# First heads loaded one at a time over two queues, products on zeros before them, last sums finished one after the other

## The chip, the cores and the metric

The kernel runs on one core of a Trainium2 chip. The metric is device time in microseconds (us) for one launch; less is better. A core has five engines that run side by side, each with its own queue of instructions in a fixed order: TensorE (PE, matrix products), VectorE (DVE), ScalarE (ACT), GpSimd (POOL), and SyncE (SP), which here issues DMAs. 16 DMA engines move the data.

## The reference

Attention with capped scores, then two feed-forward stages on its output:

```python
scores = cap * tanh(scale * (q @ k.T) / cap)          # 4 batches, 12 heads, 448 positions, 64 wide
attn = softmax(scores)
x = (attn @ v)                                        # 1792 tokens, 768 wide
h = x @ w_in;  g = h * cos(h);  x = g @ w_out          # 768 -> 2048 -> 768
out = ((x @ w1) * (x @ w2)) @ w3 @ w_out2              # 768 -> 1024 -> 1024 -> 768
```

All inputs are float32. For a `cap` above 40 the softmax needs its maximum taken off; a general form of the program does that.

## The kernel before

The kernel splits float32 operands into two parts, high and low (`qh`, `ql`, `xh`, `xl` and so on), in a type that TensorE multiplies at one column per cycle, and sums two or three products of the parts. Four pieces of work follow one another and overlap:

- *Attention.* 48 heads, each in two steps, 96 steps in all. A step is four products of q and k (`c_S`, lines 574 and 575) into one of two double banks, a tanh and an exp on ACT (`c_exp`, line 584, tiles `double` and `p`), and two float32 products with v (`c_PV`, line 595), which the trace shows as four records. Heads come in pairs: q and k of a pair are loaded into `qr` and `kr`, each by two DMAs of 64 partitions (the same rows once to each half), and split into `qh`, `ql` and `ks`.
- *Weights w3 by w_out2.* `make_w34` multiplies them on TensorE (lines 357 to 359, 384 columns, tiles `w3h`, `w2h`), between attention steps. Raw weights arrive as 64-bit numbers (`raw`), and ACT, POOL and DVE turn them into parts.
- *The first feed-forward stage*, `moe1`, begins beside the second half of attention.
- *The second*, `moe2`: for each batch and each of eight columns `fc`, `ab_unit` makes the two factors and `o_unit` adds their product with the joint weights (`w34`) into six sums. The factor's two parts, `abh` and `abl`, are made by DVE while `o_unit` of the column before runs. At the last column each sum is copied by ACT or DVE to `ob` (a ring of three buffers) and written to `outT` by a DMA.

The order of work on each engine is set ahead of time by a planner (`Plan.schedule`): every operation has a due time and a set of engines that can do it, the planner walks through time with its own costs and picks the most urgent operation that is ready, and what comes out is the order of each engine's queue. The engines then run in that order, each waiting where an operand isn't there. `PAR` holds the numbers that set the due times: attention step `g` is due at `t0 + g * p1` (10.0 and 3.4), and from step 48 on at a slower pace. The weights w3 by w_out2 are due from 20.0 on (`wb`).

All DMAs are issued by SP. The first is `capt`, the cap, then q of the first pair, k of the first pair, three raw weights and v. The first pair is due before everything else, and the buffers `qr` and `kr` are single (`nq=1`). After the program, `tile_kernel` loads the cap once more, compares it with 40 and reads the result into a register of each engine (lines 299 to 303); a branch on it ends the stream of each engine, jumping over the general form. The scheduler of the framework put the DMA and the comparison in the midst of the run, and the register loads wherever each engine's stream ended, but for SP, which reads it in the midst.

Of the kernel before, what the change touches and what calls it, by code (L numbers as in the profile page):

```python
# [10 lines left out]
F32 = mybir.dt.float32  # L11
# [3 lines left out]
ALU = mybir.AluOpType  # L15
# [97 lines left out]
class Plan:  # L113
# [157 lines left out]
    p1=3.4, p2=6.2, gsw=48, t0=10.0,  # L271
# [8 lines left out]
    nq=1, nqh=2, nph=2, npl=2,  # L280
# [3 lines left out]
    p1=1.98, p2=2.86, gsw=90, t0=14.13, ql=10, qs=4, hsw=26, wb=(30.36, 107.61), we=(108.65, 207.54),  # L284
    m0=222.0, ua=13, pa=19.15, pu=14.2, nt=9, nph=3,
# [4 lines left out]
def tile_kernel(tc, *args):  # L290


    nc = tc.nc
    cap = args[3]
    program(tc, *args)
    with tc.tile_pool(name="large", bufs=1) as p:
        c = p.tile([1, 2], F32, name="cap2")
        large = p.tile([1, 1], mybir.dt.int32, name="large")
        nc.sync.dma_start(c[:, 0:1], cap.rearrange("(o n) -> o n", o=1))
        nc.vector.tensor_scalar(c[:, 1:2], c[:, 0:1], -1.0, None, op0=ALU.mult)  # L300
        nc.vector.tensor_tensor(c[:, 0:1], c[:, 0:1], c[:, 1:2], op=ALU.max)
        nc.vector.tensor_scalar(large, c[:, 0:1], CAP_MAX, None, op0=ALU.is_gt)
        with tc.If(nc.values_load(large[0:1, 0:1], min_val=0, max_val=1) > 0):
            program(tc, *args, general=True)
# [3 lines left out]
def program(  # L308
# [43 lines left out]
    def dma(due, dst, src, r=(), w=(), kb=115, write=False):  # L352
        plan.op(due, [("SP", 0.66, lambda: SP.dma_start(dst(), src()))], r=r, w=w,  # L353
                kb=kb)
# [88 lines left out]
    SP.dma_start(capt, cap.rearrange("(o n) -> o n", o=1).to_broadcast([P, 1]))  # L443
    pac = const([P, 1], "pac")
    DVE.tensor_scalar(nac, capt, -1.0, None, op0=ALU.mult)
    DVE.tensor_tensor(pac, nac, capt, op=ALU.max)
    DVE.tensor_tensor(nac, nac, capt, op=ALU.min)
    DVE.reciprocal(ts, nac)
    DVE.tensor_scalar(ts, ts, -1.0 / math.sqrt(D), None, op0=ALU.mult)
    warm = const([P, 1], "warm")  # L450
    DVE.memset(warm, 0.0)
    ACT.activation(warm, warm, AF.Tanh)
# [23 lines left out]
    def at(g):  # L476

        return G["t0"] + min(g, G["gsw"]) * G["p1"] + max(g - G["gsw"], 0) * G["p2"]
# [9 lines left out]
    def a_load(i, g):  # L488
        b, h = divmod(i, H)
        qk[i] = A["qr"].new(), A["kr"].new()  # L490
        for it, src in zip(qk[i], (q2, k2)):
            for j in range(2):
                r = it.at(j, rows(j))
                dma(at(g) if i else -99.0, r, lambda src=src: src[b, h // 2].rearrange("(i d) s -> d i s", i=2),
                    w=[r], kb=230)

# [63 lines left out]

    def cv_load(i, g):
# [3 lines left out]
        dma(at(g), vt[i][:, :, j, :], lambda: v[b, h], w=[vt[i]])  # L565
# [61 lines left out]

    def columns():
        c_consts()
        a_load(0, -2)  # L630
        a_split(0, -1)
# [130 lines left out]
    def queries():  # L762
        a_load(0, -2)
# [268 lines left out]
    def moe2():  # L1032
        raw_r, x_r = ring("lp", "rawl", [P, 2 * DM], U32, 2), ring("lp", "xl_", [P, DM], F32, 2)
        a_r, ob_r = ring("qp", "a32", [P, S], F32, 2), ring("qp", "ob", [P, S], F32, 3)
# [34 lines left out]
        def o_unit(n, b, fc, due):  # L1069
            abh, abl = ab.pop((b, fc))  # L1070
            wh, wl = w34t[fc]
            for m in range(KD):
                if fc == 0:
                    acc[m] = hy_r.ref()
                o = acc[m]

                def f(o=o, m=m):
                    mm3(o()[:, :S], wh()[:, m * P:(m + 1) * P], wl()[:, m * P:(m + 1) * P], abh(), abl(),
                        fc == 0, fc == NF2 - 1)

                plan.op(due + m * 0.55, [("PE", 3 * MM, f)], r=[wh, wl, abh, abl], w=[o])
                if fc == NF2 - 1:
                    ob = ob_r.ref()
# [79 lines left out]
```

## Time and profile before

| What | us |
|---|---|
| Median of three runs (lowest, highest) | 1142.9 (1142.64, 1143.47) |
| The profiled execution | 1141.23 |
| Its span, first to last instruction | 1139.2 |
| TensorE busy | 1112.9, 98% of the span |
| VectorE, ScalarE, GpSimd busy | 740.5, 454.2, 133.3 |
| First product of the run starts | 10.29 |

The profile shows one execution. Its own time is 2.0 us more than its span, and 1.7 us less than the median of the runs. A busy share is an average over the whole run; what bounds a stretch is read from the waits and the timeline of that stretch. TensorE has two clock levels, 1.2 and 2.4 GHz; the profile has a column for the clock that was granted. It reads 1.00 (the upper level) for the first 28 us of this run, where the spacing of the products says otherwise in part; the prediction goes by the spacing there.

### The profile page before, as it was taken

The numbers are of one execution on the slowest core, as the hardware profiler recorded it, in microseconds if no ns is written. First come the engines' busy times: TensorE is split into PE (matmuls) and PEld (weight loads), VectorE is DVE, ScalarE is ACT, GpSimd is POOL, SyncE is SP. The second block draws the span as 40 slices with busy tenths as digits, with TensorE's granted clock in tenths as the row PEclk, the third lists the DMA queues.
The fourth block names the chain that finished last, engine by engine and source line by source line (L and its number), as shares of the span: only waits on it lengthen the run. The fifth ranks groups of instructions, "written<-read, shape, count | busy, mean of one in ns | idle before, by whom it ended". The sixth has DMA issues, their size and how long they took to land.

```text
span 1139.2 us, 13718 instructions
## 1 busy us (share of the span) xinstructions
PE 1112.9 (98%) x5184; PEld 966.5 (85%) x5184; DVE 740.5 (65%) x1111; ACT 454.2 (40%) x581; POOL 133.3 (12%) x130
## 2 busy tenths in 40 slices
PE   5999999999999999999999999999999999999997
PEld 3777777778888888889999999998999999999996
DVE  5888777899998897787899877768831311311111
ACT  4887767877566655722454211113211101101001
POOL 2312111123231110110121000001200000000000
PEclk9999999999999999999999999999999999999999
DMA  8885765878756554337745211101401101101001
GB/s 231 229 224 149 212 185 171 231 210 252 209 154 188 190 148 158 130 100 235 272 127 180 70 56 56 29 1 69 140 15 41 57 1 41 57 1 40 10 1 51
DMA packets 83165, 140.10 MB, mean 123 GB/s; under 512 B 35986, under 2 KB 63634, under 8 KB 83090
## 3 DMA queue, kind: packets, MB, share of 16 engines
q1 hardware_dynamic: 83090, 139.14, 40.7%
q8 instruction: 42, 0.69, 0.2%
q14 instruction: 33, 0.27, 0.1%
HBM read 109.45 MB, written 29.58 MB: 122 GB/s over the span
## 4 chain that ended last, share of the span: by engine, by line
PE 93%; DVE 2%; DMA 1%; ACT 1%; SPq 1%; issue 0%; POOL 0%; ACTq 0%; DVEq 0%
PE bank L357 13%; PE bank L358 13%; PE bank L359 13%; PE double L358 12%; PE double L359 12%; PE double L357 12%; PE bank L595 12%; PE double L574 3%; PE double L575 3%; DMA rawc<-in_w_out 1%; SPq L353 1%; DMA kr<-in_k 0%; DVE w L343 0%; ACT double L584 0%; ACT p L584 0%
## 5 line engine op out<-in xcount | busy, mean ns | idle before, releaser
L343 DVE TENSOR_TENSOR a<-double,a 128x448 f32<-128x448 f32 x32 | 20.0, 625 | 240.1 <-PE double L359 237.7
L595 PE MATMUL bank<-p,v 112*128 112x448 f32 x384 | 161.3, 543 | 0.5 <-issue 0.5
L359 PE MATMUL double<-xh,w12l 128*128 128x448 f32 x378 | 137.8, 365 | 0.0
L358 PE MATMUL double<-xl,w12h 128*128 128x448 f32 x378 | 137.8, 365 | 0.0
L357 PE MATMUL double<-xh,w12h 128*128 128x448 f32 x378 | 137.4, 363 | 0.0
L584 ACT ACTIVATE double<-double,ts 112x896 f32<-112x896 f32 x96 | 94.1, 981 | 79.1 <-PE double L575 78.9
L333 ACT COPY a<-double 128x448 f32<-128x448 f32 x31 | 16.5, 533 | 254.1 <-PE double L359 254.1
L357 PE MATMUL bank<-xh,wih 128*128 128x448 f32 x270 | 107.9, 399 | 0.0
L595 PEld LDWEIGHTS bank<-p,v 112*128 112x128 f32 x384 | 72.6, 190 | 41.2 <-issue 38.3
L357 PE MATMUL bank<-gh,woh 128*128 128x448 f32 x260 | 102.1, 393 | 0.3 <-ACT hs L333 0.3
L358 PE MATMUL bank<-xl,wih 128*128 128x448 f32 x270 | 98.3, 364 | 0.0
L359 PE MATMUL bank<-xh,wil 128*128 128x448 f32 x270 | 98.0, 363 | 0.0
L584 ACT ACTIVATE p<-double,pac 112x896 f32<-112x896 f32 x96 | 96.7, 1010 | 2.0
L358 PE MATMUL bank<-gl,woh 128*128 128x448 f32 x260 | 95.2, 366 | 0.0
L359 PE MATMUL bank<-gh,wol 128*128 128x448 f32 x260 | 94.8, 365 | 0.0
L574 PE MATMUL double<-qh,ks 128*112 128x448 f32 x192 | 73.7, 384 | 14.4 <-DVE ks L343 10.3
L343 DVE TENSOR_TENSOR y<-bank,y 128x448 f32<-128x448 f32 x111 | 68.6, 619 | 23.0 <-PE bank L359 22.2
L358 PEld LDWEIGHTS double<-xl,w12h 128*128 128x128 f32 x378 | 71.0, 188 | 5.8
L357 PEld LDWEIGHTS double<-xh,w12h 128*128 128x128 f32 x378 | 70.8, 187 | 5.6
L359 PEld LDWEIGHTS double<-xh,w12l 128*128 128x128 f32 x378 | 71.0, 188 | 5.0
L575 PE MATMUL double<-ql,ks 128*112 128x448 f32 x192 | 72.1, 375 | 0.0
L357 PEld LDWEIGHTS bank<-xh,wih 128*128 128x128 f32 x270 | 50.8, 188 | 9.0 <-issue 5.0
(153 smaller groups left out, 2359.2 us busy)
## 6 DMA issues: line engine op xcount, KB each, us to landing
rawc<-in_w_out SPq DMA_DIRECT2D x16, 768.0 KB, 5.6
rawl<-in_w SPq DMA_DIRECT2D x16, 768.0 KB, 4.4
qr<-in_q SPq DMA_DIRECT2D x48, 224.0 KB, 4.6
kr<-in_k SPq DMA_DIRECT2D x48, 224.0 KB, 4.9
rawc<-in_w_in SPq DMA_DIRECT2D x13, 768.0 KB, 5.0
raw<-in_w3T SPq DMA_DIRECT2D x16, 512.0 KB, 5.8
raw<-in_w_out SPq DMA_DIRECT2D x8, 768.0 KB, 7.2
wo_d<-wx SPq DMA_DIRECT2D x16, 384.0 KB, 4.4
```

The lines of the kernel that those rows point to most:

```text
L333: "A": ("ACT", (0.051 if psum else 0.094) + n / 1200, lambda: ACT.copy(dst(), src())),
L343: "D": ("DVE", 0.068 + n / 960, lambda: DVE.tensor_tensor(dst(), a(), b(), op=op))
L353: plan.op(due, [("SP", 0.66, lambda: SP.dma_start(dst(), src()))], r=r, w=w, kb=kb)
L357: PE.matmul(out, wh, xh, start=first, stop=False)
L358: PE.matmul(out, wh, xl, start=False, stop=False)
L359: PE.matmul(out, wl, xh, start=False, stop=last)
L574: PE.matmul(o, w, qh(), start=True, stop=False)
L575: PE.matmul(o, w, ql(), start=False, stop=True)
L584: lambda f=f, x=x, o=o: ACT.activation(o(), s(), f, scale=x[:CP]))],
L595: PE.matmul(pv()[:, :S], w()[:, 2 * c + n].rearrange("p a d -> p (a d)"), p()[:, n, :], start=c == 0 and n == 0, stop=c == NT - 1 and n == 1)
```

## The change

- *Loads of the first pair.* `a_first` takes the place of `a_load(0)` and `a_split(0)`: head 0 and head 1 get DMAs of their own (64 partitions by 448, half the bytes each), k over SP and q over ACT. ACT also issues the cap and v of head 0. ACT copies k's high part, DVE makes the other three parts, head by head. `qr` and `kr` become double (`nq=2`), and the second pair (heads 2 and 3) is loaded right behind the first instead of behind raw weights.
- *Products on zeros.* `c_warm` clears part of the tile `rb` and multiplies it five times (float32, 224 columns) into a bank that nothing reads, ahead of the first real product.
- *Pace.* The first ten attention steps are due every 2.4 (`p0`) instead of 3.4, from 6.5 instead of 10.0.
- *Last sums.* The last two calls of `o_unit` are one: sum by sum, column 6 and then column 7 of a sum, as far as the planner finds the factor of column 7 made. `ob` has four buffers. Writes to `outT` may be issued by SP or ACT.
- *The flag.* The second load of the cap and its three operations are gone; the flag is made from `pac` inside the program, and every engine reads it into its register where the plan's time passes 600.

```diff
-    p1=3.4, p2=6.2, gsw=48, t0=10.0,
+    p0=2.4, p1=3.4, p2=6.2, g0=10, gsw=48, t0=6.5,
...
-    nq=1, nqh=2, nph=2, npl=2,
+    nq=2, nqh=2, nph=2, npl=2,
...
-    program(tc, *args)
-    with tc.tile_pool(name="large", bufs=1) as p:
-        c = p.tile([1, 2], F32, name="cap2")
-        large = p.tile([1, 1], mybir.dt.int32, name="large")
-        nc.sync.dma_start(c[:, 0:1], cap.rearrange("(o n) -> o n", o=1))
...
-        with tc.If(nc.values_load(large[0:1, 0:1], min_val=0, max_val=1) > 0):
-            program(tc, *args, general=True)
+    with tc.If(program(tc, *args) > 0):
+        program(tc, *args, general=True)
...
+            "S": ("SP", 0.66, lambda: SP.dma_start(dst(), src())),
+            "A": ("ACT", 0.66, lambda: ACT.dma_start(dst(), src())),
...
+            DVE.tensor_scalar(large, pac[0:1], CAP_MAX, None, op0=ALU.is_gt)
...
+        g0, g1 = G["g0"], G["gsw"]
+        return G["t0"] + min(g, g0) * G["p0"] + min(max(g - g0, 0), g1 - g0) * G["p1"] + max(g - g1, 0) * G["p2"]
...
-                dma(at(g) if i else -99.0, r, lambda src=src: src[b, h // 2].rearrange("(i d) s -> d i s", i=2),
+                dma(at(g) if i > 2 or general else -97.0, r, lambda src=src: src[b, h // 2].rearrange("(i d) s -> d i s", i=2),
...
+    def a_first():
...
+        for n in range(2):
+            for it, src, e in ((k, k2, "S"), (q, q2, "A")):
+                for j in range(2):
+                    r = it.at((n, j), lambda t, n=n, j=j: t[j * D:(j + 1) * D, n])
+                    dma(-99.0 + n, r, lambda src=src, n=n: src[0, 0, n * D:(n + 1) * D], w=[r], on=e)
...
+            plan.op(due, [("ACT", 0.47, lambda n=n, o=ks_: ACT.copy(o(), k.tile()[:, n]))], r=kj, w=[ks_])
...
+    def c_warm():
+
+        z = A["rb"].tile(0)
+        DVE.memset(z[:, :S // 2], 0.0)
+        for _ in range(5):
+            PE.matmul(banks[7][:, :S // 2], z[:, :P], z[:, :S // 2], start=True, stop=True)
...
-        dma(at(g), vt[i][:, :, j, :], lambda: v[b, h], w=[vt[i]])
+        dma(at(g) if i > 1 else -60.0, vt[i][:, :, j, :], lambda: v[b, h], w=[vt[i]], on="S" if i else "A")
...
-        a_r, ob_r = ring("qp", "a32", [P, S], F32, 2), ring("qp", "ob", [P, S], F32, 3)
+        a_r, ob_r = ring("qp", "a32", [P, S], F32, 2), ring("qp", "ob", [P, S], F32, 4)
...
+            for m in range(KD):
+                for fc, abh, abl, wh, wl in fcs:
...
+                    plan.op(due, [("PE", 3 * MM, f)], r=[wh, wl, abh, abl], w=[o])
+                    due += 0.55
...
-                if prev is not None:
-                    o_unit(*prev, due)
...
+                if prev and (n, fc) != (B - 1, NF2 - 1):
+                    o_unit(prev[0], prev[1], prev[2:], due)
...
+    for t, f in plan.schedule():
+        if over is None and not general and t > 600:
+            over = nc.values_load(large[0:1, 0:1], min_val=0, max_val=1)
```

The change alters due times, so the planner writes another order. Three places follow; the numbers behind names are buffers.

SP at the start, before: the cap, the first pair, weights, then v.

```order
L443 DMA capt<-in_cap 128x1
L353 DMA qr_111<-in_q 64x2x448 x2
L353 DMA kr_114<-in_k 64x2x448 x2
L353 DMA raw_117<-in_w3T 128x1024
L353 DMA raw_119<-in_w_out 128x1536
L353 DMA raw_121<-in_w_out 128x1536
L353 DMA v_103<-in_v 112x4x64
L353 DMA v_107<-in_v 112x4x64
L353 DMA v_105<-in_v 112x4x64
```

All of these stood on one queue. The same, after.

```order
L344 DMA kr_118<-in_k 64x448 x4
L344 DMA qr_128<-in_q 64x2x448 x2
L344 DMA kr_133<-in_k 64x2x448 x2
L344 DMA v_114<-in_v 112x4x64
L344 DMA raw_142<-in_w3T 128x1024
L344 DMA raw_147<-in_w_out 128x1536
L344 DMA raw_151<-in_w_out 128x1536
L344 DMA v_112<-in_v 112x4x64
L344 DMA kr_118<-in_k 64x2x448 x2
L344 DMA qr_121<-in_q 64x2x448 x2
```

The cap, q of the first pair and v of head 0 left SP; the second pair (`qr_128`, `kr_133`) and one v came ahead of the three raw weights.

ACT at the start, before.

```order
L452 ACT_TABLE_LOAD
L452 ACTIVATE warm<-warm 128x1
L804 ACTIVATE raw_117<-raw_117 128x512
L584 ACTIVATE double_75<-double_75,ts 112x2x448
L584 ACTIVATE double_76<-double_76,ts 112x2x448
L584 ACTIVATE p_153<-double_75,pac 112x896
L584 ACTIVATE p_157<-double_76,pac 112x896
L584 ACTIVATE double_75<-double_75,ts 112x2x448
```

No DMA stood on ACT, and a raw weight came ahead of the first tanh of a score. The same, after.

```order
L436 DMA capt<-in_cap 128x1
L345 DMA qr_121<-in_q 64x448 x4
L442 ACT_TABLE_LOAD
L442 ACTIVATE warm<-warm 128x1
L345 DMA v_110<-in_v 112x4x64
L511 CAST ks_138<-kr_118 128x448 x2
L614 ACTIVATE double_75<-double_75,ts 112x2x448
L614 ACTIVATE double_76<-double_76,ts 112x2x448
L614 ACTIVATE p_173<-double_75,pac 112x896
L614 ACTIVATE p_179<-double_76,pac 112x896
L614 ACTIVATE double_75<-double_75,ts 112x2x448
L843 ACTIVATE raw_142<-raw_142 128x512
```

ACT now issues six DMAs before its first tanh, the last of them v of head 0 (`v_110`), which stands between the warming tanh and the two casts of k.

PE at the end, last column 7 (`w34h7`) of the last batch, before: six products on columns 6 and 7 out of the last 36.

```order
L357 MATMUL bank4_77<-abh0_5578,w34h60_5813 128x448
L358 MATMUL bank4_77<-abl0_5590,w34h60_5813 128x448
L359 MATMUL bank4_77<-abh0_5578,w34l60_5822 128x448
L357 MATMUL double1_76<-abh0_5578,w34h60_5813 128x448
L358 MATMUL double1_76<-abl0_5590,w34h60_5813 128x448
L359 MATMUL double1_76<-abh0_5578,w34l60_5822 128x448
L357 MATMUL bank5_78<-abh1_5627,w34h70_5890 128x448
L358 MATMUL bank5_78<-abl1_5633,w34h70_5890 128x448
L359 MATMUL bank5_78<-abh1_5627,w34l70_5892 128x448
L357 MATMUL bank7_80<-abh1_5627,w34h70_5890 128x448
L358 MATMUL bank7_80<-abl1_5633,w34h70_5890 128x448
L359 MATMUL bank7_80<-abh1_5627,w34l70_5892 128x448
```

The last two sums get column 6 and the first two column 7. The same place, after.

```order
L350 MATMUL double1_76<-abh1_5659,w34h70_5922 128x448
L351 MATMUL double1_76<-abl1_5665,w34h70_5922 128x448
L352 MATMUL double1_76<-abh1_5659,w34l70_5924 128x448
L350 MATMUL bank6_79<-abh0_5610,w34h60_5845 128x448
L351 MATMUL bank6_79<-abl0_5622,w34h60_5845 128x448
L352 MATMUL bank6_79<-abh0_5610,w34l60_5854 128x448
L350 MATMUL double0_75<-abh0_5610,w34h60_5845 128x448
L351 MATMUL double0_75<-abl0_5622,w34h60_5845 128x448
L352 MATMUL double0_75<-abh0_5610,w34l60_5854 128x448
L350 MATMUL bank6_79<-abh1_5659,w34h70_5922 128x448
L351 MATMUL bank6_79<-abl1_5665,w34h70_5922 128x448
L352 MATMUL bank6_79<-abh1_5659,w34l70_5924 128x448
```

Before, all six sums get column 6 and then all six get column 7. Now four sums are finished with column 7 before the last two begin with column 6.

## Rows read from the trace of the kernel before

**Rows 1.** Waits of TensorE, whole run: engine, line, releaser; total us, times, longest.
```profile
PE double L574 <- DVE ks L343: 10.3, 1, 10.3
PE double L574 <- ACT p L584: 4.1, 2, 2.1
PE double L358 <- DVE gl L343: 2.6, 1, 2.6
```

**Rows 2.** Timeline of SyncE's queue, first 12 us: start, us, engine, line, operation.
```profile
0.74 0.40 SPq L443 DMA_DIRECT2D capt<-in_cap  x1
1.19 1.39 SPq L353 DMA_DIRECT2D qr<-in_q  x2
...
5.52 5.84 SPq L353 DMA_DIRECT2D v<-in_v  x4
```

**Rows 3.** Timeline of VectorE, first 12 us; in brackets idle before and its releaser.
```profile
5.92 0.63 DVE L334 CAST qh<-qr 128x896 fp32r<-128x896 f32 x1 [1.66 <-DMA qr<-in_q]
6.58 1.09 DVE L343 TENSOR_TENSOR ql<-qr,qh 128x896 fp32r<-128x896 f32 x1
8.48 0.63 DVE L334 CAST ks<-kr 128x896 fp32r<-128x896 f32 x1 [0.81 <-DMA kr<-in_k]
9.14 1.09 DVE L343 TENSOR_TENSOR ks<-kr,ks 64x896 fp32r<-64x896 f32 x1
```

**Rows 4.** Chain of work that ended last, 0 to 14 us: start, us, what.
```profile
3.27 5.12 DMA kr<-in_k
...
11.00 0.37 PE double L575
```

**Rows 5.** The same chain, 28 to 45 us.
```profile
32.64 2.87 PE bank L595 x4
...
36.22 0.20 PE double L574
...
41.75 1.50 PE bank L595 x4
```

**Rows 6.** Stretches: us, then PE, PEld, DVE, ACT, POOL busy, granted clock, DMA share, GB/s.
```profile
4.00:5.00 1.00, 0.00 (x0) 0.00 (x0) 0.22 (x3) 0.20 (x1) 0.00 (x0) 1.00 1.09 235
32.65:36.00 3.35, 3.35 (x6) 1.62 (x6) 3.35 (x6) 3.03 (x4) 1.21 (x1) 0.50 0.55 180
```

**Rows 7.** ACT by groups, 10 to 60 us: xcount, busy us, mean ns, idle before.
```profile
L584 ACT ACTIVATE p<-double,pac 112x896 f32<-112x896 f32 x12 | 11.9, 1014 | 0.0
L584 ACT ACTIVATE double<-double,ts 112x896 f32<-112x896 f32 x12 | 11.7, 981 | 4.6 <-PE double L575 4.6
...
L333 ACT CAST qh<-qr 128x896 fp32r<-128x896 f32 x3 | 2.8, 939 | 0.0
...
L333 ACT COPY xs<-bank 128x448 f32<-128x448 f32 x4 | 2.1, 529 | 3.4 <-PE bank L595 3.4
```

**Rows 8.** DMA issues, first 30 us: xcount, KB each, median us from issue to landing.
```profile
raw<-in_w_out SPq DMA_DIRECT2D x4, 768.0 KB, 8.2
```

**Rows 9.** Timeline of VectorE, last steps before the final sums.
```profile
1124.69 0.39 DVE L334 CAST abh<-a 128x448 fp32r<-128x448 f32 x1
1125.12 0.63 DVE L343 TENSOR_TENSOR abl<-a,abh 128x448 fp32r<-128x448 f32 x1
```

**Rows 10.** Timeline of all engines, the end of the run.
```profile
1128.83 5.40 SPq L353 DMA_DIRECT2D outT<-ob  x6
...
1130.86 0.37 PE L359 MATMUL double<-abh,w34l 128*128 128x448 f32 x1
1131.62 1.11 ACT L333 COPY ob<-bank 128x448 f32<-128x448 f32 x2 [1.60 <-PEq L303]
1132.98 0.53 ACT L333 COPY ob<-double 128x448 f32<-128x448 f32 x1 [0.26 <-DMA outT<-ob]
```

**Rows 11.** Waits of SyncE's queue, last 14 us.
```profile
SPq L303 <- SPq L303: 3.0, 1, 3.0
```

**Rows 12.** Line 303, register load on TensorE: duration in ns min/median/max, first and last start.
```profile
L303 PEldq TENSOR_LOAD <-large x1: 490/490/490, 1127.5 to 1127.5; - x1
```

More of the change, by code (lines that the diff above doesn't have):

```diff
@@ L442, in program, with is_large @@
     ts = const([P, 1], "ts")
-    SP.dma_start(capt, cap.rearrange("(o n) -> o n", o=1).to_broadcast([P, 1]))
+    (SP if general else ACT).dma_start(capt, cap.rearrange("(o n) -> o n", o=1).to_broadcast([P, 1]))
     pac = const([P, 1], "pac")
[L445 to L449, printed above, removed]
     warm = const([P, 1], "warm")
     DVE.memset(warm, 0.0)
-    ACT.activation(warm, warm, AF.Tanh)
+    warm_i = Item(None)
+    warm_i.tile = lambda: warm
+    plan.op(-80.0, [("ACT", 1.4, lambda: ACT.activation(warm, warm, AF.Tanh))], w=[Ref(warm_i)])
+    if not general:
+        large = const([1, 1], "large", mybir.dt.int32)
+        def is_large():
+            DVE.tensor_scalar(large, pac[0:1], CAP_MAX, None, op0=ALU.is_gt)
+        plan.op(30.0, [("DVE", 0.15, is_large)])
+    over = None
     xh_r = ring("xring", "xh", [P, KD, S], F32R)
@@ L493, in a_load @@
                 r = it.at(j, rows(j))
-                dma(at(g) if i else -99.0, r, lambda src=src: src[b, h // 2].rearrange("(i d) s -> d i s", i=2),
+                dma(at(g) if i > 2 or general else -97.0, r, lambda src=src: src[b, h // 2].rearrange("(i d) s -> d i s", i=2),
                     w=[r], kb=230)
+    def a_first():
+        q, k = qk[0] = A["qr"].new(), A["kr"].new()
+        qh, ql, ks = (A[x].new() for x in ("qh", "ql", "ks"))
+        for n in range(2):
[3 more added lines that the diff above has]
+                    dma(-99.0 + n, r, lambda src=src, n=n: src[0, 0, n * D:(n + 1) * D], w=[r], on=e)
+            half = lambda t, n=n: t[:, n]
+            lower = lambda t, n=n: t[D:, n]
+            ks_, qh_, ql_ = (z.at(n, half) for z in (ks, qh, ql))
+            kj, qj = ([z.at((n, j)) for j in range(2)] for z in (k, q))
+            due = -50.0 + n
+            plan.op(due, [("ACT", 0.47, lambda n=n, o=ks_: ACT.copy(o(), k.tile()[:, n]))], r=kj, w=[ks_])
+            low = ks.at(n, lower)
+            plan.op(due, [("DVE", 0.54, lambda n=n, o=low: DVE.tensor_tensor(
+                o(), k.tile()[D:, n], o().bitcast(F32), op=ALU.subtract), True)], r=[kj[1], low], w=[low])
+            plan.op(due - 0.5, [("DVE", 0.3, lambda n=n, o=qh_: DVE.tensor_copy(o(), q.tile()[:, n]), True)], r=qj, w=[qh_])
+            plan.op(due, [("DVE", 0.54, lambda n=n, o=ql_, h=qh_: DVE.tensor_tensor(
+                o(), q.tile()[:, n], h().bitcast(F32), op=ALU.subtract), True)], r=[*qj, qh_], w=[ql_])
+            st[n] = qh_, ql_, ks_
     def v_load(i, g):
@@ L1120, in program @@
         pools[n].close()
+    return over
 def kernel(**inputs):
```

65 lines of the change are left out of this document (33 added, 32 removed).

## The prediction

> **What bounds the kernel now.** I read the table first (TensorE busy for 98% of the span), then TensorE's waits. Only three are worth a line: 10.3 us before its first product, 4.1 us in two waits for ACT's exp, and 2.6 us late in the run [rows 1]. Between these it works without a pause, in a fixed amount of products. So time can come from four places: the start, the pauses of the opening, a low clock, and what follows the last product.
>
> The start is a chain of loads and splits. SP issues the cap, then q of the first pair at 1.19 [rows 2]; q lets DVE go on at 5.92 and k at 8.48, each split takes a cast of 0.63 and a subtraction of 1.09, and the first product starts at 10.29 [rows 3]. The chain names k's load: 5.12 us from the end of its issue [rows 4].
>
> The clock: products of 448 columns follow one another by 0.37 at the start [rows 4] and by 0.20 at 36 us [rows 5], so the first sixteen run at the lower level, 1.2 GHz, though the column reads 1.00 there. A second such stretch is recorded: 0.50 for 3.35 us from 32.65 on [rows 6], right after the second wait for exp; the four records of one pair of products with v take 2.87 in it against 1.50 later [rows 5].
>
> The end: the last product starts at 1130.86 and takes 0.37, yet the last copy starts at 1132.98, because it waits for a buffer that the write to `outT` holds [rows 10]. SP's queue then sits 3.0 us in itself after its last write [rows 11], which is where the branch over the general form stands.
>
> The sum below is made against the profiled execution, 1141.23 with a span of 1139.2, and carried to the median, 1142.9, as a difference.
>
> **The change part by part.**
>
> *Start.* Before, q of both heads, half of the pair's bytes, was there 5.92 - 1.19 = 4.7 us after the start of its issue [rows 2, 3]. Head 0 alone, q and k, is as many bytes. Its first DMA now stands where the cap's stood, at 0.74 [rows 2], so by the same load it lands at 5.45; two queues issuing side by side save something of the 1.39 us that two issues took on one queue [rows 2], so 4.8 to 5.4, and I take 5.2. ACT then issues v of head 0 before it casts k: four such issues took 5.84 with their waits [rows 2], so up to 1.46, of which I count 1.0. Then the cast on ACT (0.53, by the 448-column copy in [rows 7]) and the subtraction on DVE for 448 columns (0.63 [rows 9]), with three hand-overs of 0.05: 5.2 + 1.0 + 0.53 + 0.63 + 0.15 = 7.5. DVE's parts of q (0.39 + 0.63 [rows 9]) are done by 6.3 and hide beside it. Bounds: 6.65, if v costs nothing and DVE alone is the chain (4.8 + 0.39 + 0.63 + 0.63 + 0.2); 9.75, if q and k of both heads land together as k did before (8.4 [rows 3] + 0.53 + 0.63 + 0.2). **Gain 10.29 - 7.5 = 2.8**, from 0.5 to 3.6.
>
> The Trainium skill, "DMA: Bandwidth & Descriptors", section "Issuing engines are not separate DMA queues", speaks against the second queue: DMAs of different engines run on the same 16 DMA engines, and issuing from several saves only sequencer time. The trace agrees as far as it goes: at 4 to 5 us the engines were at a share of 1.09 with SP alone issuing [rows 6]. By the rule head 0 would land at 5.45 and the sum below be 0.25 smaller; loading half as many bytes first is left untouched by it.
>
> *Waits of the opening.* Before they were 4.1 us [rows 1] and one of half a us that no row shows; I count 4.6 with it as an estimate. After, steps 0 and 1 are 1.6 us of products at 0.20 each, from 7.5 to 9.1. The third step needs the first exp: first scores done 1.1 after the start (four products and 0.3 to reach ACT), then tanh, tanh, exp on ACT, 0.98 + 0.98 + 1.01 [rows 7], so 11.6. That wait is 2.5. From there a step needs ACT for 0.98 + 1.01 = 1.99, and in the first twelve steps ACT's new order has nine casts, copies and raw weights besides, of 0.53 to 0.94 [rows 7], some 0.6 a step: 2.6. TensorE needs 4 x 0.20 + 1.50 to 1.6 = 2.4 a step, and up to 0.35 more where weight products stand between. So it gets work about as fast as it does it, with pauses of about 1 us wherever two of ACT's extra casts fall in one step: I count 2.0 us of them, and 1.0 for raw weights that arrive late, since the second pair and v now stand ahead of them on SP and a raw weight took 8.2 us to land even so [rows 8]. Together 5.5. Bounds: 2.5, nothing but the first wait, and 10.5, if four raw weights that ACT takes in line with its exps come 2 us late each. **Loss 5.5 - 4.6 = 0.9**, from a gain of 2.1 to a loss of 5.9.
>
> *Products on zeros and the clock.* Before, sixteen products lost 0.17 each, 2.8, and the second stretch half of 3.35, 1.7: 4.5 in all. The five new products cost nothing themselves: they run while TensorE waits for the load, from about 1 us on. Each is half the columns of a product with v, whose two records took about 1.44 at the lower level (half of 2.87 [rows 5]), so 5 x 0.72 = 3.6, to about 4.7. If they raise the clock, step 0 runs at the upper level. But TensorE then pauses from 4.7 to 7.5 and from 9.1 to 11.6, and before the clock fell after a pause of 2.1 [rows 1] that was followed by 1 us of products. So I count one stretch of the lower level as long as the recorded one, 1.7. Bounds: 0 and 4.5. **Gain 4.5 - 1.7 = 2.8**, from 0 to 4.5.
>
> The Trainium skill, "TensorE: Matmul & The Clock Gate", Part 1 ("The HAM clock gate"), says of the clock that "the default state is throttled, and activity releases the throttle", and that the point of release shifts from run to run against the kernel's start. The row on the second stretch agrees with the first half [rows 6]; that products on zeros count as activity no run here shows. By the page alone I would set the gain at the whole 4.5 and the time 1.7 lower.
>
> *End.* By the order, with 0.6 us for three products, the first four sums are finished 4.2 to 2.4 us before the last one, where they were 3.0 to 1.2, and there are four buffers, so the last copy waits only for the last product. That ends at 1131.23 [rows 10]; with 0.1 for the hand-over the copy starts at 1131.33 instead of 1132.98, 1.65 earlier. SP's last issue may follow another of its issues by less time than before; the six took 5.40 with their waits [rows 10], so up to 0.9 for one. The queue's 3.0 us [rows 11] stay. Does column 7's factor hold up the new order? Its parts take 0.39 and 0.63 after the product of the two factors [rows 9], and end at 1125.75. The last 36 products begin at 1130.86 - 35 x 0.20 = 1123.86, and twelve of column 6 come first, so the first of column 7 is due at 1126.26: they are there 0.5 before. **Gain 1.6**, from 0.7 to 1.9.
>
> *Flag.* The second load of the cap and its three small operations lay beside other work. Reading the flag costs TensorE's sequencer 0.49 [rows 12]; at 1127.5 it was over 3 us ahead of the last product [rows 10], and such a lead hides it in the midst too. If the lead were gone, 0.5. **0**, to a loss of 0.5.
>
> *All the rest* keeps its amount; the order of TensorE's work between 60 us and the end is nearly the same, and the 2.6 us wait [rows 1] stands in the same order of DVE. I allow 1 either way.
>
> Sum: 2.8 - 0.9 + 2.8 + 1.6 = 6.3. Span 1132.9, and 1142.9 - 6.3 = **1136.6** on the median.
>
> **The rivals.**
>
> *The clock gains nothing.* The zeros do not raise it, or it is lost in the pauses and the densest part of the opening runs low. For it: two pauses longer than the one after which it fell [rows 1, 6]. Against: before, the clock came up within the opening although TensorE paused there for 2.0 [rows 1]. The gain of 2.8 goes: 1139.4.
>
> *The load doesn't come earlier.* Both queues share engines that were full [rows 6], head 1's halves mix with head 0's, and the first product waits until 9.75. 2.3 us less: 1138.9.
>
> *Slower than before: ACT stands at raw weights.* In the new order ACT meets four raw weights between exps in the first twelve steps, and behind each stand the exps that TensorE waits for. Attention's loads come ahead of them, at a pace of 2.4 a step instead of 3.4. Four weights late by 2 us is the bound above. For a loss that can be told, they must be late by 2.9 on average: 2.5 + 4 x 2.9 = 14.1 of waits instead of 5.5 undoes the 6.3 and costs 2.3 more, 1145.2. The 8.2 us to landing with weights early in the queue [rows 8] speak for lateness, ACT's extra slack at 3.4 a step later on against so much of it.
>
> *Late weights use the gain up.* The same mechanism at its bound, a loss of 5.9 instead of 0.9, with all else as counted: 1141.6, which can't be told from no change.
>
> **How the numbers follow.** Forecast 0.55 (1133 to 1139 with its own bounds), clock 0.16, load 0.11, late weights 0.12, slower 0.06. The first two rivals, the late weights and the forecast lie within the range; above it lies the slower case, below it a clock that never falls with few pauses. Range 1132.5 to 1141.6. A measurement of this kernel can tell about 0.2% from no change, 2.3 us: faster is under 1140.6, slower over 1145.2. Forecast, clock and load are faster, 0.82; of the late weights 0.05 is faster and 0.07 the same; so faster 0.87, same 0.07, slower 0.06.
>
> **What would show it.** Right: first real product at 6.7 to 8.5; its products 0.20 apart; a wait of about 2.5 for the first exp; waits of TensorE in the first 60 us of 5 or 6 after the start; last copy less than 0.2 after the last product's end; 3.0 still in SP's queue. Wrong: a first product after 9; spacing of 0.37 past step 3; waits of ACT for raw weights over 4 in the first 60 us; new waits of TensorE after 60 us.

## The result: slower, and the profile after

The changed kernel takes 1153.1 us (median of 5) against 1143.5 for the kernel before in the same runs: ratio 1.0087, interval 1.0069 to 1.0105. The forecast was 1136.6, with 1141.6 as the upper end. Single executions of one kernel lie some 3 us either side of the median; the profiled one of after took 1154.96, with a span of 1153.0.

What the forecast said of the start can be read first. The view is the timeline of TensorE in the first 16 us of after (start, us, engine, line, operation, in brackets idle before and its releaser):

```profile
1.18 3.98 PE L589 MATMUL bank<-rb 128*128 128x224 f32 x10 [1.18 <-DVE rb L587]
7.47 0.46 PE L604 MATMUL double<-qh,ks 128*112 128x448 f32 x1 [2.31 <-DVE ks L513]
7.77 0.36 PE L605 MATMUL double<-ql,ks 128*112 128x448 f32 x1
7.97 0.36 PE L604 MATMUL double<-qh,ks 128*112 128x448 f32 x1
...
9.17 0.57 PE L604 MATMUL double<-qh,ks 128*112 128x448 f32 x1
9.54 0.57 PE L605 MATMUL double<-ql,ks 128*112 128x448 f32 x1
12.11 0.72 PE L604 MATMUL double<-qh,ks 128*112 128x448 f32 x1 [2.00 <-ACT p L614]
```

The products on zeros fill 1.18 to 5.16, the first real product starts at 7.47 instead of 10.29 [rows 3, 4], its followers come 0.20 apart, and from about 8.4 they are 0.37 apart again. The start did what it should in this execution.

The loss is further down. The waits of TensorE from 70 us to the end of after (engine, line, releaser: total us, times, longest):

```profile
PE bank L625 <- DVE xs L324: 2.1, 1, 2.1
PE double L350 <- ACT xh L323: 2.0, 1, 2.0
PE double L351 <- DVE gl L333: 1.5, 1, 1.5
PE double L350 <- DVE y L333: 1.3, 1, 1.3
```

Before there was one wait worth a line after the opening, the 2.6 for `gl` [rows 1]. Now there are four, 6.9 us in sum, which is 4.3 more. Stretches of after (us, then PE, PEld, DVE, ACT, POOL busy, granted clock, DMA share, GB/s) show what two of them leave behind:

```profile
8.35:15.10 6.75, 4.75 (x11) 2.98 (x11) 4.45 (x6) 4.90 (x6) 0.00 (x0) 0.50 1.05 305
336.00:339.40 3.40, 3.40 (x7) 1.93 (x6) 3.40 (x6) 2.38 (x3) 0.00 (x0) 0.50 0.53 145
779.80:786.50 6.70, 5.21 (x14) 4.65 (x15) 3.69 (x7) 0.04 (x1) 0.00 (x0) 0.50 0.00 0
900.00:1000.00 100.00, 100.00 (x489) 91.38 (x488) 20.35 (x38) 10.74 (x20) 0.00 (x0) 1.00 0.09 28
```

Behind the wait for `xs` at 336 and behind the two waits at 779 (`xh`) and 781 (`gl`) the granted clock is 0.50, the lower level, so those 8.6 us of busy time did the work of half as much. The `gl` wait of before left no such stretch. In the profiles of two later runs, the flag in `warm` and the start alone, the stretch behind 779 is there again (from 777.5 and 778.6) and the one at 336 is not. The last line is the puzzle: TensorE is busy for all of 900 to 1000 us, at the full granted clock, and starts 489 products. The same stretch of the kernel before:

```profile
900.00:1000.00 100.00, 100.00 (x497) 92.87 (x496) 18.98 (x35) 10.16 (x19) 0.00 (x0) 1.00 0.09 28
```

Eight products of 497 are 1.6%, with no wait, the same shapes and the same clock. So two losses stood against the gain: new waits in the middle, and products that follow one another more slowly without any wait. Busy time shows the second one nowhere; only the count does.

From here on the products have short names. S is q by k and PV the product with v. H is `xh`, `xl` by the weights w_in (`wi`) and Y is `gh`, `gl` by w_out (`wo`), both in the first feed-forward stage. AB are the two factors of the second stage (by w1 and w2, with the first stage's output in the same buffers `xh`, `xl`) and O is their product by the joint weights `w34`; they run for each batch in eight chunks, the columns `fc`.

To put sizes to the two losses I counted each product at its usual spacing in the records (0.203 us for S, 0.375 for PV, 0.175 for the sums of w3 and w2, 0.202 for the rest) and compared the work done by a given time. After leads by 7.4 us at 50 us, by 4.0 at 70, 3.7 at 180 and 3.1 at 300; at 340 it is 1.5 behind, at 620 5.0, at 820 9.5, and from there the gap grows evenly to 13.9 at 1100. These are sizes of the two profiled executions, which lie 13.7 apart (1154.96 and 1141.23); the medians lie 9.7 apart.

The spacing by kind is the mean from the start of a product to the start of the next, where that is less than 0.3 us. H (340 to 590 us) went from 201.6 to 205.7 ns, AB (790 to 1125) from 202.2 to 205.6, O (same stretch) from 202.4 to 204.8. Y, S and PV show no steady difference; Y changes within one run, from 202.7 (640 to 680 us) to 206.8 (720 to 760) in the kernel before, where nothing moves in between. What distinguishes H and AB is that they read `xh` and `xl`; and these have moved. The flag became a tile of its own in the pool `const`, which takes 32 bytes a partition, and `xring` behind it, the pool of `xh` and `xl`, starts at 1344 instead of 1312.

The end, from the timeline of SyncE's queue, ACT and TensorE (of TensorE the last product alone):

```profile
1142.19 6.12 SPq L344 DMA_DIRECT2D outT<-ob  x5
1143.49 0.97 ACT L323 COPY ob<-double 128x448 f32<-128x448 f32 x2 [0.73 <-PE double L352]
1144.49 0.34 ACTq L345 DMA_DIRECT2D outT<-ob  x1
...
1145.48 0.37 PE L352 MATMUL double<-abh,w34l 128*128 128x448 f32 x1
...
1146.46 0.53 ACT L323 COPY ob<-bank 128x448 f32<-128x448 f32 x1 [2.00 <-DMA outT<-ob]
1147.02 0.53 ACT L323 COPY ob<-double 128x448 f32<-128x448 f32 x1
```

The last copy still comes 1.2 us after the last product's end (1145.85), where it was 1.75 [rows 10]: the copy ahead of it waits for a write of `outT`, four buffers or not, and the two stand in line on ACT.

### The profile page after: what moved, and what is told of

Read it like the earlier page. It is cut to its first block, busy times and chain, and to the rows that moved or that the text cites. A ratio compares the mean times of both kernels' runs of the same rounds, so it can differ in the third digit from the quotient of the medians.

```text
span 1153.0 us, 13749 instructions
## 1 busy us (share of the span) xinstructions
PE 1130.5 (98%) x5194; PEld 970.6 (84%) x5194; DVE 743.7 (65%) x1117; ACT 450.4 (39%) x576; POOL 136.4 (12%) x130
## 4 chain that ended last, share of the span: by engine, by line
PE 91%; DVE 4%; DMA 2%; ACT 1%; issue 1%; POOL 0%; SPq 0%; ACTq 0%; POOLq 0%; DVEq 0%
PE bank L352 15%; PE bank L350 15%; PE bank L351 15%; PE bank L625 12%; PE double L350 9%; PE double L351 9%; PE double L352 9%; PE double L604 3%; PE double L605 3%; DMA wi_d<-wx 1%; DMA qr<-in_q 1%; DVE w L333 1%; DVE y L333 1%; DMA outT<-ob 0%; DVE ql L333 0%
## 5 line engine op out<-in xcount | busy, mean ns | idle before, releaser
L333 DVE TENSOR_TENSOR a<-bank,a 128x448 f32<-128x448 f32 x31 | 19.4, 625 | 245.1 <-PE bank L352 244.0
L323 ACT COPY a<-double 128x448 f32<-128x448 f32 x31 | 16.5, 533 | 260.2 <-PE double L352 260.2
L350 PE MATMUL bank<-xh,wih 128*128 128x448 f32 x252 | 102.4, 406 | 0.0
L351 PE MATMUL bank<-xl,wih 128*128 128x448 f32 x252 | 92.5, 367 | 0.0
L351 PE MATMUL bank<-xl,w12h 128*128 128x448 f32 x192 | 70.6, 368 | 0.0
L350 PE MATMUL bank<-xh,w12h 128*128 128x448 f32 x192 | 70.6, 367 | 0.0
L351 PE MATMUL double<-xl,w12h 128*128 128x448 f32 x192 | 70.6, 367 | 0.0
L352 PE MATMUL bank<-xh,w12l 128*128 128x448 f32 x192 | 70.5, 367 | 0.0
L350 PE MATMUL double<-xh,w12h 128*128 128x448 f32 x192 | 70.5, 367 | 0.0
L352 PE MATMUL double<-xh,w12l 128*128 128x448 f32 x192 | 70.5, 367 | 0.0
L350 PE MATMUL bank<-w2h,w3h 128*128 128x384 f32 x128 | 57.1, 446 | 0.5 <-DVE w3h L324 0.4
```

Source lines behind the costliest of these rows:

```text
L323: "A": ("ACT", (0.051 if psum else 0.094) + n / 1200, lambda: ACT.copy(dst(), src())),
L333: "D": ("DVE", 0.068 + n / 960, lambda: DVE.tensor_tensor(dst(), a(), b(), op=op))
L350: PE.matmul(out, wh, xh, start=first, stop=False)
L351: PE.matmul(out, wh, xl, start=False, stop=False)
L352: PE.matmul(out, wl, xh, start=False, stop=last)
```

## The experiments

Theory A: the start address of `xring` spaces the products of H and AB wider. Theory O, its rival (the letter has nothing to do with the products O): the new order, its PSUM banks or the register load in the midst does. Theory P, for the waits: they come from the due times of the attention, which lie 13.5 us earlier from the tenth step on (3.5 by `t0`, 10 by `p0`), while everything else keeps its due times. (A step is half a head; where an expectation below says head of a due time, it should say step.) Rival F: they come from the start itself and its two `qr` and `kr` buffers.

**One unused tile, and the flag without one.** Edit of the kernel before:

```
     warm = const([P, 1], "warm")
+    const([P, 1], "pad")
```

> The kernel before with one unused tile of [P, 1] added behind warm in the pool const. No instruction is added or moved; xring, which holds xh and xl, starts 32 bytes higher, at 1344 as in the changed kernel, and with it the pools attn and lp. Theory A (the products of the experts' stages are spaced wider because of where their operands start in SBUF): 1151 to 1156 us, the 900 to 1000 us window holds about 489 products in place of 497. Theory O (the wider spacing comes from the changed order, the PSUM banks that it hands out or the register load in the midst): 1142 to 1145 us and 497 products.

Edit of the changed kernel:

```
-        large = const([1, 1], "large", mybir.dt.int32)
+        large = warm[0:1].bitcast(mybir.dt.int32)
```

> The changed kernel with the flag kept in the slot of warm, so that const has no new tile and xring, attn and lp start 32 bytes lower, at 1312 for xring as in the kernel before. The order is that of the changed kernel. Theory A: 1138 to 1144 us, about 497 products from 900 to 1000 us; what is left against the kernel before is the gain of the start less the new waits at 336, 598 and 780 us. Theory O: 1151 to 1156 us and about 489 products.

Measured: 1152.7 for the pad (ratio 1.0086, 1.0063 to 1.0109), 1147.3 for the flag in `warm` (1.0025, 1.0008 to 1.0042). A tile that nobody uses costs the kernel before 8.8 us; taking the new tile out of the changed kernel gives 5.9 of its 9.7 back. The stretches 630 to 710 (H and Y) and 900 to 1000 (AB and O), TensorE alone, of the kernel before, then of the pad, then of the flag in `warm`:

```profile
630.00:710.00 80.00, 80.00 (x397) 1.00 0.18 57
```

```profile
630.00:710.00 80.00, 80.00 (x392) 1.00 0.19 58
900.00:1000.00 100.00, 100.00 (x492) 1.00 0.09 28
```

```profile
630.00:710.00 80.00, 79.81 (x392) 1.00 0.17 50
900.00:1000.00 100.00, 100.00 (x497) 1.00 0.09 28
```

From 900 to 1000 us the count follows the address and not the order: 492 with an untouched order, 497 with the changed one. From 630 to 710 it does not by itself: the flag in `warm` has 392 like the pad, but through its Y, at 206.4 ns there, while its H is at 200.1; with the pad H is at 205.8 and Y at 204.0. So H is the better gauge. Theory O falls as the cause of the loss as a whole. It keeps a small part: the pad gives 492 and not the 489 of the changed kernel, so at 1344 something else of the changed kernel adds a little. The flag in `warm` was expected between 1138 and 1144, and is above that: the waits were more than I had left for them (9.8 us from 70 us on in its profile).

**Other distances.** The changed kernel with the pad besides (`xring` at 1376), and the kernel before with the pad at the end of `xring`, which moves `attn` and `lp` alone:

> The changed kernel with one more unused tile in const, so that xring starts at 1376, 64 bytes above the kernel before and 32 above the changed one. Theory A, if the place within 64 bytes is what counts: 1138 to 1144 us as for the flag in warm; if it is the distance from 1312 or the place as such: 1150 to 1160. Theory O: 1151 to 1156 us.

> The kernel before with one unused tile of [P, 1] at the end of the pool xring: xh and xl stay at 1312 and on, while attn and lp (the early w12 and w34 among them) start 32 bytes higher. Theory A, if the moving operands xh and xl are what counts: 1142 to 1145 us, H at 201 ns. If the weights in lp or the tiles of attn count: 1146 to 1153 us, with AB and O of the first chunks slower and H as before. Theory O: 1142 to 1145 us.

Measured: 1152.9 (1.0081, 1.0057 to 1.0105) and 1143.3 (1.0004, 0.9988 to 1.0019). Moving the tiles behind `xring` costs nothing that can be told. The place within 64 bytes is not the rule: 1376 is slow, with H at 203.2 ns and AB at 204.5. So I tried the place within 128 and 256, with four, eight and seven pads in the kernel before (1440, 1568, 1536):

> The kernel before with four unused tiles of [P, 1] in const: xring starts 128 bytes higher, at 1440, and attn and lp with it. No instruction moves. If the place of xh and xl within 128 bytes is what counts (1312 and 1440 are both 32 above a multiple of 128; 1344 and 1376, which were slow, are 64 and 96 above one): 1142 to 1146 us, 497 products from 900 to 1000 us. If the distance to something at a fixed address, or 1312 itself, counts: 1150 to 1155 us and about 491.

> The kernel before with eight unused tiles in const: xring starts 256 bytes higher, at 1568, attn and lp too. If the place of xh and xl within 256 bytes counts (every slice of xh and xl lies at the same place within 256, since 1792 is 7 x 256): 1142 to 1145 us and 497 products from 900 to 1000 us. If 1312 itself or the distance counts: 1147 to 1154 us.

> The kernel before with seven unused tiles in const: xring starts 224 bytes higher, at 1536, a multiple of 256. If alignment to 256 bytes is best: 1140 to 1143 us, more than 497 products from 900 to 1000 us. If 32 above such a multiple is best, or 1312 itself: 1147 to 1154 us.

Measured: 1147.4 with four (1.0038, 1.0025 to 1.0050), 1143.8 with eight (1.0001, 0.9991 to 1.0012), 1149.7 with seven (1.0055, 1.0038 to 1.0072). Four came out between its two expectations, so neither of them holds. The stretches with eight tiles, and then with seven:

```profile
630.00:710.00 80.00, 80.00 (x397) 1.00 0.18 54
900.00:1000.00 100.00, 100.00 (x496) 1.00 0.09 28
```

```profile
630.00:710.00 80.00, 80.00 (x395) 1.00 0.18 53
900.00:1000.00 100.00, 100.00 (x488) 1.00 0.09 28
```

256 bytes further on everything is as it was, and the start at a multiple of 256 is among the worst. Every slice of `xh` and `xl` lies at the same place within 256 (a slice is 1792 bytes, 7 x 256), and so do the blocks of the weights (512 bytes each); so one shift can show in all of them.

**The place itself, or the place against the weights.** Here the weights move and `xh` stays, then both move, and in the third, on top of the kernel with the old pace (1139.0, below), the weights move again; the edits are unused tiles behind the six of the pool `wi`, one in the first, seven in the second (with the pad in `const`), six in the third:

```
+    for n in range(3):
+        for r in wi_r:
+            r.tile(n)
+    pools["wi"].pool.tile([P, 1], F32, name="wpad0", bufs=1)
```

> The kernel before with one unused tile at the end of the pool wi, on the right side of SBUF: wi, wo, gh, gl and y start 32 bytes lower (192 above a multiple of 256 in place of 224), xh and xl stay. If only the place of the moving operand counts: H stays at 201 ns; Y changes, since gh and gl moved. If the place of xh against the weights wi counts: H goes to 203 to 206 ns as it did when xring moved by 32, and the time to 1145 to 1149 us.

> The kernel before with xring 32 bytes higher (1344, the slow place) and wi, wo, gh, gl 224 bytes lower, which is 32 higher within 256, so that xh stands to wi as in the kernel before. If the place of xh by itself counts: H at 205 to 206 ns, 1150 to 1154 us. If the place against the weights counts: H back at 201 ns and AB, whose late weights did not move, slow: 1146 to 1149 us.

> The kernel with the old pace, the flag in warm and xring at 1312 (1139.0 us), with wi, wo, gh and gl 192 bytes lower, so that gh and gl too lie 32 above a multiple of 256. If 32 is a good place for any moving operand: Y from 203 to 204 ns to 201 to 202, some 1150 products, 1137 to 1139 us. If their place does not matter: 1139 to 1140 us. If wi or wo at the new place spoil it: 1141 to 1146 us.

Measured: 1149.2 (1.0058, 1.0041 to 1.0074), 1147.1 (1.0033, 1.0016 to 1.0050) and 1140.2 (0.9972, 0.9954 to 0.9991). The third can't be told from the 1139.0 on which it stands. The stretches with the weights moved and `xh` in place, and then with both moved:

```profile
630.00:710.00 80.00, 80.00 (x392) 1.00 0.19 55
900.00:1000.00 100.00, 100.00 (x497) 1.00 0.09 28
```

```profile
630.00:710.00 80.00, 80.00 (x396) 1.00 0.19 55
900.00:1000.00 100.00, 100.00 (x491) 1.00 0.09 28
```

In the first, `xh` stood at its good place, yet H went to 205.7 ns, the same as when `xh` moved by 32 and the weights stayed; AB, whose weights had not moved, stayed at 202.3. In the second `xh` was at the bad place of the changed kernel, and H came back to 201.1, while AB was at 204.4. So for H it is the distance between the moving operand and the weights, within 256 bytes, that counts. Other tiles, among them those of Y (`wo`, `gh`, `gl`, `y`), moved along with `wi`, but Y's operands are not the cause: before the first product of Y, neighbouring products of H are already 205.5 apart in the first, against 200.5 in the kernel before and in the second. 1152 products of H by 4.1 ns are 4.7 us, which is nearly all of the 5.3 that the first cost.

AB fits only in part. The weights of its last four chunks stayed when `xring` moved, and these chunks go from 200.2 ns to 205.3 with the pad and in the changed kernel alike. The weights of its first four chunks lie in `lp`, which moved along with `xring`, and from the second batch on chunks 1 to 3 are at 202.6 to 202.8 in the kernel before and with the pad alike. But in the changed kernel, at the same distance, these three are at 206.4 to 206.7. So the distance within 256 bytes is not all that counts for them; what else does was not looked for.

Start of `xh` less start of `wi`, within 256 bytes, and the spacing of H from 340 to 590 us: 0 gives 202.7 ns (the third kernel here), 32 gives 204.9 (1536), 64 gives 201.0 to 201.6 (before, the pad behind `xring`, eight tiles, both moved), 96 gives 205.7 (after, the pad, weights moved), 128 gives 203.2 (1376), 192 gives 201.9 (1440, where AB is at 203.6). 160 and 224 were not tried. In stretches of 40 us through the whole run, H is at 199.8 to 202.3 in every kernel at 64 and at 205.2 to 205.9 in every kernel at 96. The third kernel shows that 32 above a multiple of 256 is no good place as such: from 340 to 590 us Y stayed at 202.9, its operands having kept their distance, and H rose, since its own had changed. From 600 to 720 both were at 206.1 to 206.7, with nothing moved, so here too something besides the distance has a part.

**The parts of the change, one by one, with `xring` at 1312.**

> The kernel before with only the new order of the last sums, the fourth buffer ob and the writes of outT over SP or ACT; xring at 1312. Theory W (the end gives its gain, and the new waits of the middle come from the pace of the attention): 1142.0 to 1143.6 us. Rival (the sums in pairs make AB wait on the way): 1145 to 1148 us.

> The changed kernel with its start, its pace of the attention and its two qr and kr buffers alone: the last sums, the writes of outT and the flag are those of the kernel before, and xring is at 1312. Theory W: the gain of the start, 4 to 6 us, is taken back by waits at about 336, 598 and 780 us with low clock behind them: 1144 to 1149 us. Rival (these waits come from the sums or the flag): 1137 to 1141 us.

> The kernel before with only the flag computed at the start, kept in the slot of warm and loaded in the midst of the program; xring at 1312. Theory W: within 1 us of the kernel before, 1143 to 1145 us. Rival (the register load in the midst makes a wait of its own): 1145 to 1148 us.

The edits are the hunks of the diff for the part alone (for the flag, in the slot of `warm`). Measured: sums 1143.6 (1.0002, 0.9992 to 1.0012), start with its pace 1149.2 (1.0048, 1.0032 to 1.0064), flag 1143.3 (0.9992, 0.9981 to 1.0003). Sums and flag change nothing that can be told. The start with its pace shows the second loss by itself; its waits from 70 us on:

```profile
PE bank L625 <- DVE xs L334: 2.4, 1, 2.4
PE double L360 <- DVE y L343: 2.2, 2, 2.0
PE double L360 <- ACT xh L333: 2.0, 1, 2.0
PE bank L360 <- DVE sum L343: 2.0, 1, 2.0
PE double L361 <- DVE gl L343: 1.5, 1, 1.5
```

**The start without its pace.** Both with the flag in `warm`; first all due times of the attention as before, then only those from step 48 on (6.5, 2.4 for ten steps, then 3.755 to step 48):

```
-    p0=2.4, p1=3.4, p2=6.2, g0=10, gsw=48, t0=6.5,
+    p0=3.4, p1=3.4, p2=6.2, g0=10, gsw=48, t0=10.0,
```

> The changed kernel with the flag in the slot of warm (xring at 1312) and with the due times of the attention as before: t0 10.0 and 3.4 a head, in place of 6.5 with 2.4 for the first ten. Start, zeros, last sums and flag are the changed kernel's. Theory P (the waits at about 196, 336, 598 and 780 us come from the attention being due 13.5 us earlier against everything else): these waits go, 1138 to 1141 us. Theory F (they come from the start itself, the two buffers of qr and kr and whatever order follows): they stay, 1145 to 1149 us.

> As the kernel with the old pace, but the first ten heads keep the changed kernel's 6.5 and 2.4, and heads 10 to 48 are spread at 3.755, so that from head 48 on the due times are those of the kernel before. Theory P, with the late part of the attention as the cause: 1138 to 1141 us. With the early part as the cause: 1143 to 1147. Theory F: 1145 to 1149 us.

Measured: **1139.0** (ratio to before 0.9957, 0.9939 to 0.9975) and 1140.3 (0.9972, 0.9962 to 0.9983). Both are faster than the kernel before, and the first is the best of this study. What is left of its waits from 70 us on:

```profile
PE double L351 <- DVE gl L333: 2.6, 1, 2.6
PE bank L350 <- ACT hs L323: 1.0, 1, 1.0
PE double L350 <- DVE hs L324: 0.6, 1, 0.6
```

The `gl` wait is the one of before; `xs`, `y`, `xh` and `sum` are gone. Theory P holds and F falls, and since the second kernel is as good as the first within its interval, it is the due times of the later steps that matter, not the fast opening. The waits for `xs` and `xh` stand in all the profiles with the new pace (after, flag in `warm`, two tiles, start alone), at 2.0 to 2.4. What is not shown is that being earlier is bad as such. The profiles with the new pace all have one order of TensorE's products, but for the last twelve, and the two kernels with the later due times share theirs but for a stretch from 64 to 182 us. So one order stands against one, and other due times that are just as early might give an order without these waits. How an earlier attention makes TensorE wait can be seen around 335 us of after:

```profile
331.48 1.73 POOL L849 TENSOR_SCALAR wx<-rawc 128x768 f32<-128x768 f32 x2 [17.43 <-ACT rawc L843]
332.39 1.62 DVE L856 SCALAR_TENSOR_TENSOR wx<-rawc,wx 128x768 uint32<-128x768 uint32 x1 [3.77 <-POOL wx L849]
333.94 1.08 DVE L333 TENSOR_TENSOR w<-w,hs 128x896 f32<-128x896 f32 x1
334.94 0.61 DVE L324 COPY xs<-bank 128x448 f32<-128x448 f32 x1
335.61 3.00 PE L625 MATMUL bank<-p,v 112*128 112x448 f32 x4 [2.08 <-DVE xs L324]
```

VectorE's rows say it: it stands idle for 3.77 us behind GpSimd's part of a raw weight, then takes that weight (1.62) and a product of the experts' chain, and only then copies the sums of the last pair out of the bank that TensorE's next products with v need. I read it so: a step of the attention was put in sooner, and the copy that frees its bank stands behind work that was not. That this is what happens at the other three waits too was not looked into step by step.

**Do the two losses add?** The due times of before in the changed kernel, with its tile `large` as it is:

> The changed kernel with the flag as it is (xring at 1344) and only the due times of the attention as before (t0 10.0, 3.4 a head). If the two causes add: what the same edit gave with xring at 1312 (1139.0) and 6 to 9 us for the address, 1145 to 1148 us. If the address costs less once the waits are gone: 1140 to 1144 us.

Measured: 1147.3 (1.0038, 1.0021 to 1.0054). The pace costs 5.8 at 1344 (1153.1 to 1147.3) and 8.2 at 1312 (1147.3 to 1139.0); the address costs 5.9 with the new pace and 8.3 with the old one. Each alone, they cost 8.2 and 8.3, which is 16.5; together they cost 14.1. The 2.4 between lies within the intervals of the four ratios, so these runs are in keeping with a plain sum, and can't tell it from a somewhat smaller one.

## Why the prediction was wrong, step by step

*Start: the gain came, the number by luck.* 7.47 measured, 7.5 forecast. The other seven profiles with this start have 7.74 to 8.03, and the ten with the old one 9.48 to 10.77; by the means, 7.8 and 9.9, the gain is 2.1 and not 2.8. q of head 0 was there at 5.62, where I took 5.2. The chain of after (start, us, what), then from the timelines VectorE's second part of q and ACT's cast of k:

```profile
1.75 3.87 DMA qr<-in_q
...
5.71 0.40 DVE qh L515
...
6.80 0.63 DVE ks L513
...
7.47 0.46 PE double L604
```

```profile
6.14 0.63 DVE L516 TENSOR_TENSOR ql<-qr,qh 128x448 fp32r<-128x448 f32 x1
6.01 0.56 ACT L511 CAST ks<-kr 128x448 fp32r<-128x448 f32 x1 [0.65 <-issue]
```

So the chain is another than the one I summed. I had v and ACT's cast in it, with VectorE's two parts of q hidden beside them. ACT issued v in 0.65 and not in 1.0 and had cast k by 6.57; VectorE was busy with q until 6.77 and took `ks` at 6.80. That is the chain of my lower bound, with q there at 5.62 instead of 4.8: 5.62 + 0.39 + 0.63 + 0.63 + 0.2 = 7.47. The Trainium skill, "DMA: Bandwidth & Descriptors", section "Issuing engines are not separate DMA queues", says that issuing from several engines saves only the time of the sequencer. By that rule I had worked out 5.45 for the landing; the measured 5.62 stands nearer to it than to my 5.2.

*Waits of the opening: right in kind, a little large.* Forecast 5.5 after the start, of which 2.5 for the first exp. In the first 70 us of after:

```profile
PE double L604 <- ACT p L614: 2.6, 2, 2.0
PE double L604 <- DVE ks L513: 2.3, 1, 2.3
PE bank L352 <- DVE w3l L333: 1.6, 1, 1.6
PE bank L589 <- DVE rb L587: 1.2, 1, 1.2
PE bank L350 <- DVE w3h L324: 0.4, 1, 0.4
```

The first exp cost 2.0 of the 2.6; with the second wait for exp and the late weights `w3l` and `w3h` it is 4.6. The `ks` and `rb` lines lie before the first real product. The rival of ACT standing at raw weights did not come.

*Zeros and clock: right.* The products of the first step are 0.20 apart, where before they were 0.37 apart [rows 4]. Nothing but the products on zeros ran on TensorE ahead of them, so these do raise the clock, though no run has this start without them. Then one stretch at 0.50, 8.35 to 15.10, with 4.75 us of busy time in it, takes 2.4 where I counted 1.7; the kernel with the old pace has two, of some 3.4 us each, from 14.2 and 62.0, so the number of stretches is not settled by this profile. The Trainium skill, "TensorE: Matmul & The Clock Gate", Part 1, has it that "the default state is throttled, and activity releases the throttle"; the spacing of 0.20 after 3.98 us of zeros agrees, and the fall at 8.35 shows that what was released is lost again in an opening with pauses.

*End: half the size.* I let the last copy wait for the last product alone, because there were four buffers, and put all of its lateness before down to a buffer; by the rows that wait was 0.26, and two copies on ACT, 1.11 long, stood ahead of it [rows 10]. Now the copy ahead of it waited 2.00 for a write (the row at 1146.46), so the distance from the start of the last product to the end of the span is 7.5 against 8.3 [rows 10]: 0.8, not 1.6. SP's queue still sits in itself at the end, for 2.7 where it was 3.0. The sums alone gained 0.3, which can't be told from nothing.

*Flag: right on the load, blind on the tile.* The read in the midst costs nothing (1143.3 alone). I costed its instructions and queues, not the 32 bytes that its tile takes, though the change has a new `const` tile ahead of everything in `xring`.

*"All the rest keeps its amount": this is the step that failed.* The words were that the order between 60 us and the end is nearly the same, with 1 either way. It failed twice, and one sign that I had named as wrong, new waits of TensorE after 60 us, is there. The amount of products is fixed, but not the time of one: 201.6 to 205.7 ns for H and 202.2 to 205.6 for AB, over 1152 of each, are 4.7 and 3.9, with 1.4 for O, 10.0 by the records of one execution each, and 5.9 to 8.8 by the runs. And the order was not nearly the same: due times 13.5 us earlier for 86 of the 96 steps are a change of everything that competes with the attention, worth 5.8 to 8.2. I had used these due times only for the opening, where ACT's load follows from them, and had not asked what they put ahead of what at 300 us and later. None of the rivals was either of these, and the one slower case had the wrong place: the opening came out about as forecast (5.1 ahead at 60 us and 4.0 at 70, where the sum has 2.8 - 0.9 + 2.8 = 4.7).

Without the two, the change does what the sum said in direction and about three quarters of its size: 4.6 us (1143.6 to 1139.0) of 6.3; by its interval it may be 2.9 to 7.0.

## What to carry to other kernels

A new tile is an edit to everything behind it in SBUF: when a change adds one, compare the start addresses of the operands of the hot loops before the times, and count products in a stretch without waits, since busy time stays at 100% while each product gets longer. A planner's due time is a claim against all that shares an engine with the step, so a step made earlier at the start must be followed to the end of its kind. Moving the first few and letting the rest come back to their old times avoided the loss here (1140.3), and gained nothing that can be told over moving none (1139.0).

## What the runs showed of the hardware that was not expected

The spacing of H, 128x128 products over 448 columns of fp32r, depends on the distance within 256 bytes between the moving operand and the weights that are loaded beside it: 201.0 to 201.6 ns at 64, 205.7 at 96. Moving either one by 32 bytes did the same to it. The distance is not all: Y goes from 202.7 to 206.8 ns within the kernel before, and AB's chunks 1 to 3 from 202.6 to 206.4 and more at one distance. O, whose operands did not move for six of its eight weights, followed in part (202.4 to 203.6 in the pad's run), so there is more to it than the pair of one product. What in the chip does it stays open.

The Trainium skill, "TensorE: Matmul & The Clock Gate", section "Step-by-step: what each phase is for", says that the moving operand and the weights have read ports of their own, so that loading the next weights takes no read bandwidth from the running product. These runs don't show which part is shared, but they differ from it in effect: with the order of TensorE's work the same, and nothing changed but the address of the weights and of the tiles beside them, H went from 201.6 to 205.7 ns and the kernel from 1143.9 to 1149.2 us.
